# One word of each row of the first raw weights is fetched ahead of everything else, with the order of all engines drawn up anew

## The chip, the cores and the metric

The kernel runs on one core of a Trainium2 chip. A core has engines with instruction queues of their own: TensorE (PE: matmuls, and PEld for its weight loads), VectorE (DVE), ScalarE (ACT), GpSimd (POOL) and SyncE (SP), which here issues every DMA. The metric is the device time of one execution in microseconds (us), the median of repeated runs. The kernel before has 666.44 us.

## What is computed

Attention between 512 tokens and 32 states per head, both ways, for 8 batches of 8 heads of width 64. Then all 4,352 rows go through a gated product: two matmuls with 512 x 1536 weights, an elementwise product, and a matmul with 1536 x 512 weights.

```python
def _attn_ref(x, state):
    scores = scale * np.matmul(x, state.transpose(0, 1, 3, 2))
    a = softmax(scores)                       # over the 32 states
    xread = np.matmul(a, state)
    scores2 = scale * np.matmul(state, x.transpose(0, 1, 3, 2))
    a2 = softmax(scores2)                     # over the 512 tokens
    sread = np.matmul(a2, x)
    return np.concatenate([xread, sread], axis=2)

def reference(x, state, moe_w_a, moe_w_b, moe_w_out):
    x = _attn_ref(x, state) as rows of 512
    return ((x @ moe_w_a) * (x @ moe_w_b)) @ moe_w_out
```

## The kernel before

Every product is kept near float32 by splitting its operands into a high and a low part of 11 to 12 bits (names ending in `_h` and `_l`) and adding three products: high by high, high by low, low by high. Weights arrive as raw 64-bit words (`wl` for the first layer, `w_out` for the second). A conversion turns each 512 KB piece of them into float32: ScalarE makes `t1` from the raw words (`pre`), and VectorE follows with two shifts with masks, a multiply-add and a sum (`Whole.run`), or with a few more where the high and low parts are wanted apart (`Conv.run`). The trace writes such tiles as `raw` or, where the buffer has another name, `sd_h` and `sd_l`, the shifted words as `t`, and converted weights as `wo`.

The start of the program is this chain, for batch 0. The tokens `x` arrive in two halves for the first four heads (`x<-xt`, two transfers of 288 KB), then in one of 576 KB for the others. `scores` multiplies them with the states into the PSUM tile `ms`. ScalarE copies that (`p_raw`), TensorE turns it back to rows of tokens (`acc<-ident,p_raw`), and VectorE takes the maximum `m` of each group and subtracts it (`s_p`). ScalarE exponentiates, VectorE adds and divides, TensorE transposes again, and ScalarE splits the result into `sd_h` and `sd_l` (batch 0 has its attention weights in these buffers; later batches in `at_h` and `at_l`). Meanwhile the four pieces of the first two chunks of `wl` are converted, and `direct` multiplies them with the states into `p_h` and `p_l`. Layer 1 (`layer1`, `product`) multiplies these with the attention weights into two PSUM tiles `ab`, and their elementwise product is `a_sb`, with parts `g_h` and `g_l`. Layer 2 multiplies `g` with `wo0`, `wo1` and so on into `acc`. From then on eight batches and twelve such pieces of the hidden width follow; the last part works with seven products in place of eight for blocks of two by two (`sevens`).

Until the first layer-1 matmul TensorE also runs 80 matmuls `ab<-y` whose result nobody reads. They fill its idle time (`WARM`, `COLD`).

The order of the instructions is not that of the code. Every call is recorded as a unit with an engine, a duration and its dependences; `plan` then simulates the engines with these costs and always starts the ready unit that is due first. Due times are worked out backwards from the end and moved by two tables of numbers found by search: `SHIFTS` moves the due time of a group of units, `RELEASES` holds a group back until a given time. The result is one fixed order on each engine, and the semaphores follow from it. The cost of a load is an issue on SP, a start-up, a time for its bytes and a fixed time to land; `Conv.load` gives the very first piece of `wl` an extra cost. Each engine runs its queue in the order planned: an instruction that waits holds up all behind it.

All instructions are issued by one line of code at the end (L1800), so in the trace they are told apart by their tiles.

Of the kernel before, what the change touches and what calls it, by code (L numbers as in the profile page):

```python
# [12 lines left out]
I32 = mybir.dt.int32  # L13
# [7 lines left out]
P = 128  # L21
# [26 lines left out]
T0, PACE = 15e3, 1.12  # L48
STARTS = {}
# [246 lines left out]
class Engine:  # L296
# [557 lines left out]
def attn_moe(ctx, tc, xt, xn, sd, wl, w_out, out):  # L854
# [20 lines left out]
    tail = pool("tail", 8)  # L875
# [41 lines left out]
    class Conv:  # L917
# [6 lines left out]
        def load(self, place):  # L924
            self.raw = load64(self.src, place, self.runs)
            if not count[0]:
                u = rec.units[-1]
                u.serve, u.land, u.lat = u.serve + 1200, u.land + 900, u.lat + 2100
# [914 lines left out]
```

## Time and profile before

| | |
|---|---|
| median of 3 runs (lowest, highest) | 666.44 us (665.91, 666.53) |
| the profiled execution | 665.95 us |
| its span, first to last instruction | 663.7 us |
| TensorE busy | 653.6 us (98%) |
| VectorE busy | 548.5 us (83%) |
| ScalarE busy | 382.0 us (58%) |
| 16 DMA engines busy, mean | 70% |
| granted TensorE clock, mean | 0.999 |

The profiled execution lies 2.25 us above its span and 0.49 us below the median of the runs. Busy time of TensorE is an upper measure, since a matmul's record overlaps the next one's by up to some 0.16 us; waits of less than that do not show as idle time. The rest is read by stage.

### The profile page before, as it was taken

The numbers are of one execution on the slowest core, as the hardware profiler recorded it, in microseconds if no ns is written. First come the engines' busy times: TensorE is split into PE (matmuls) and PEld (weight loads), VectorE is DVE, ScalarE is ACT, GpSimd is POOL, SyncE is SP. The second block draws the span as 40 slices with busy tenths as digits, with TensorE's granted clock in tenths as the row PEclk, the third lists the DMA queues.
The fourth block names the chain that finished last, engine by engine and source line by source line (L and its number), as shares of the span: only waits on it lengthen the run. The fifth ranks groups of instructions, "written<-read, shape, count | busy, mean of one in ns | idle before, by whom it ended". The sixth has DMA issues, their size and how long they took to land.

```text
span 663.7 us, 12125 instructions
## 1 busy us (share of the span) xinstructions
PE 653.6 (98%) x4451; PEld 544.9 (82%) x4451; DVE 548.5 (83%) x1219; ACT 382.0 (58%) x707; POOL 0.7 (0%) x6
## 2 busy tenths in 40 slices
PE   7999999999999999999999999999999999999997
PEld 4566777776777778888888989898989989889996
DVE  5999989998877787878989978877777879877885
ACT  4677488699989976654545543534444444424442
POOL 0000000000000000000000000000000000000000
PEclk9999999999999999999999999999999999999999
DMA  8998579889989999866876764754426217268830
GB/s 298 356 359 310 232 252 343 285 308 359 351 296 391 339 325 344 314 213 187 253 239 217 249 231 121 251 169 159 156 100 168 98 53 213 75 181 188 233 96 33
DMA packets 77242, 155.06 MB, mean 234 GB/s; under 512 B 7040, under 2 KB 26240, under 8 KB 77184
## 3 DMA queue, kind: packets, MB, share of 16 engines
q1 hardware_dynamic: 77184, 154.30, 69.7%
q8 instruction: 35, 0.57, 0.4%
q14 instruction: 23, 0.19, 0.1%
HBM read 91.36 MB, written 62.91 MB: 232 GB/s over the span
## 4 chain that ended last, share of the span: by engine, by line
PE 91%; DVE 5%; DMA 1%; ACT 1%; issue 1%; DVEq 0%
PE ab L1800 44%; PE acc L1800 39%; PE ms L1800 9%; DVE t L1800 2%; DVE wo L1800 1%; DMA x<-xn 1%; DVE m L1800 1%; DVE s_p L1800 1%; DMA x<-xt 0%; DVE stg L1800 0%; DVE p_l L1800 0%; DVE g_l L1800 0%; ACT sw_st L1800 0%; ACT g_h L1800 0%; DVE x L1800 0%
## 5 line engine op out<-in xcount | busy, mean ns | idle before, releaser
L1800 PE MATMUL acc<-wo,g_h 128*128 128x256 f32 (+1 forms) x868 | 178.8, 316 | 0.6 <-ACT stg L1800 0.3
L1800 PEld LDWEIGHTS acc<-wo,g_h 128*128 128x128 f32 x868 | 135.4, 190 | 19.9 <-issue 3.4
L1800 PE MATMUL ab<-at_l,p_h 128*128 128x512 f32 x368 | 144.5, 393 | 0.0
L1800 PE MATMUL ab<-at_h,p_h 128*128 128x512 f32 x368 | 144.4, 397 | 0.0
L1800 PE MATMUL ab<-at_h,p_l 128*128 128x512 f32 x368 | 143.2, 391 | 0.0
L1800 PE MATMUL acc<-wo,g_l 128*128 128x256 f32 (+1 forms) x587 | 127.3, 308 | 0.2
L1800 PEld LDWEIGHTS acc<-wo,g_l 128*128 128x128 f32 x587 | 93.0, 190 | 11.5 <-issue 1.2
L1800 ACT CAST g_h<-a_sb 128x512 fp32r<-128x512 f32 (+1 forms) x104 | 63.8, 613 | 56.7 <-DVE a_sb L1800 26.9
L1800 PEld LDWEIGHTS ab<-at_h,p_h 128*128 128x128 f32 x368 | 69.1, 188 | 17.5 <-issue 2.9
L1800 PEld LDWEIGHTS ab<-at_h,p_l 128*128 128x128 f32 x368 | 69.1, 188 | 15.7 <-issue 0.8
L1800 PEld LDWEIGHTS ab<-at_l,p_h 128*128 128x128 f32 x368 | 69.3, 188 | 12.1 <-issue 0.8
L1800 DVE TENSOR_TENSOR g_h<-a_sb,g_h 128x512 fp32r<-128x512 f32 x68 | 46.5, 684 | 15.8 <-PE acc L1800 11.7
L1800 ACT COPY wq<-ab 128x512 f32<-128x512 f32 (+1 forms) x48 | 27.3, 568 | 43.5 <-PE ab L1800 43.4
L1800 DVE TENSOR_TENSOR wq<-ab,wq 128x512 f32<-128x512 f32 (+1 forms) x48 | 31.9, 664 | 21.9 <-PE ab L1800 19.0
L1800 ACT CAST p_h<-p_raw 128x1024 fp32r<-128x1024 f32 x32 | 33.6, 1051 | 21.9 <-PE ab L1800 18.8
L1800 DVE TENSOR_TENSOR p_l<-p_raw,p_h 128x1024 fp32r<-128x1024 f32 x32 | 38.9, 1214 | 1.3 <-ACT p_h L1800 1.2
L1800 DVE TENSOR_TENSOR stg<-acc,stg 128x256 f32<-128x256 f32 (+1 forms) x68 | 36.3, 549 | 3.6 <-PE acc L1800 2.6
L1800 ACT CAST g_l<-wq 128x384 fp32r<-128x384 f32 x46 | 23.5, 513 | 26.6 <-PE acc L1800 23.9
L1800 DVE TENSOR_TENSOR g_l<-wq,g_l 128x384 fp32r<-128x384 f32 x46 | 25.4, 552 | 15.4 <-PE acc L1800 10.7
L1800 ACT COPY p_raw<-ms 128x512 f32<-128x512 f32 x48 | 27.6, 590 | 10.5 <-PE ms L1800 9.8
L1800 DVE TENSOR_SCALAR t<-t 128x512 int32<-128x512 int32 x64 | 26.7, 418 | 5.1 <-ACT t L1800 4.8
L1800 DVE TENSOR_TENSOR a_sb<-ab,a_sb 128x512 f32<-128x512 f32 (+1 forms) x36 | 23.6, 654 | 7.1 <-PE ab L1800 5.4
(137 smaller groups left out, 1060.0 us busy)
## 6 DMA issues: line engine op xcount, KB each, us to landing
p_raw<-scr SPq DMA_DIRECT2D x32, 512.0 KB, 4.8
raw<-wl SPq DMA_DIRECT2D x20, 512.0 KB, 5.3
out<-stg SPq DMA_DIRECT2D x33, 256.0 KB, 2.2
su<-wq SPq DMA_DIRECT2D x16, 512.0 KB, 6.0
scr<-sw_st SPq DMA_DIRECT2D x32, 256.0 KB, 4.7
scr<-p_raw SPq DMA_DIRECT2D x32, 256.0 KB, 4.7
x<-xn SPq DMA_DIRECT2D x16, 512.0 KB, 5.0
x<-xt SPq DMA_DIRECT2D x14, 512.0 KB, 6.4
```

The source lines that it names most:

```text
L1800: getattr(obj, method)(*map(real, args), **{k: real(x) for k, x in kw.items()})
```

## The change

Three things are edited. A DMA `touch<-wl` is issued first: 8 bytes of each of 128 rows of `wl[0]` (two 32-bit words, 1 KB in all) into a small tile that nobody reads. The two loads of batch 0's first tokens are recorded as users of that tile, which puts them behind it in the order, without a wait. And the planner's extra cost of the first load of weights is cut to a fifth. Both tables were then searched anew, so the order of every engine changes along the whole program.

```diff
 T0, PACE = 15e3, 1.12
+TOUCHED = True
...
 SHIFTS = {
-    0: 961, 1: 522, 2: -345, 3: -1004, 4: 175, 5: 340, 6: 86993674, 7: 86992534, 8: -40, 9: 377, 10: -272, 11:
...
         def load(self, place):
             self.raw = load64(self.src, place, self.runs)
             if not count[0]:
                 u = rec.units[-1]
-                u.serve, u.land, u.lat = u.serve + 1200, u.land + 900, u.lat + 2100
+                u.serve, u.land, u.lat = u.serve + 200, u.land + 200, u.lat + 400
...
+    touch = tail.tile([P, 2], I32, name="touch", bufs=1)
+    nc.sync.dma_start(out=touch, in_=wl[0, :, 0, :1].bitcast(I32))
...
                 if self.b == 0 and g == 0:
                     for h in range(2):
-                        nc.sync.dma_start(out=x[:, g, h], in_=xt[self.b, g, :, h])
+                        u = nc.sync.dma_start(out=x[:, g, h], in_=xt[self.b, g, :, h])
+                        u.touch.append(touch)
+                        u.acc.append((touch.tile, 0, False))
```

The instructions on TensorE, VectorE and ScalarE are the same ones before and after, in another order; SP has one DMA more. Three places show the order.

On SP, the first transfers of the program, before:

```order
L1800 DMA x<-xt 128x576 x2
L1800 DMA raw<-wl 128x1024
L1800 DMA x<-xt 128x1152
L1800 DMA raw<-wl 128x1024
L1800 DMA sd_h_122<-wl 128x1024
L1800 DMA kept_0_128<-p_raw 128x512
L1800 DMA xst<-sd 64x4x128 x2
L1800 DMA sd_l_144<-wl 128x1024
L1800 DMA x<-xt 128x2x512 x2
```

and now (the first row is the new transfer, `kept` stores the scores, `xst` are the states):

```order
L1807 DMA touch<-wl 128x2
L1807 DMA x<-xt 128x576 x2
L1807 DMA raw<-wl 128x1024 x2
L1807 DMA x<-xt 128x1152
L1807 DMA xst<-sd 64x4x128 x2
L1807 DMA kept_0_145<-p_raw 128x512
L1807 DMA sd_h_149<-wl 128x1024
L1807 DMA sd_l_164<-wl 128x1024
```

The new transfer stands first, so each `x` moves back by one issue. The third piece of weights (`sd_h<-wl`) stood ahead of the store `kept<-p_raw`, which waits for ScalarE; it now stands behind it, and the second piece has moved ahead of the third load of `x`.

On TensorE, its first rows (`ab<-y` are the matmuls that nobody reads, `ms<-x` the first scores), before:

```order
L1800 MATMUL ms<-x 32x512 x4
L1800 MATMUL ab<-y 128x256 x3
L1800 MATMUL acc<-ident,p_raw 128x128 x4
L1800 MATMUL ab<-y 128x256 x14
L1800 MATMUL ms<-x 32x512 x4
L1800 MATMUL ab<-y 128x256 x12
L1800 MATMUL acc<-ident,s_p 128x128 x4
```

and now:

```order
L1807 MATMUL ab<-y 128x256 x12
L1807 MATMUL ms<-x 32x512 x4
L1807 MATMUL ab<-y 128x256 x5
L1807 MATMUL acc<-ident,p_raw 128x128 x4
L1807 MATMUL ab<-y 128x256 x10
L1807 MATMUL ms<-x 32x512 x4
L1807 MATMUL ab<-y 128x256 x13
L1807 MATMUL acc<-ident,s_p 128x128 x4
```

Twelve of the unread matmuls now stand ahead of the first scores; before, TensorE began with the scores.

On VectorE, its 48th to 58th instructions, around the first two products `a_sb` of layer 1 (`wo_413` and `wo_403` are the same piece of weights under two numbers), before:

```order
L1800 TENSOR_TENSOR a_sb<-ab,a_sb 128x512
L1800 TENSOR_TENSOR wo_413<-wo_413,t_399 128x512
L1800 TENSOR_SCALAR t_428<-t_417 128x512
L1800 TENSOR_SCALAR wo_413<-t_417 128x512
L1800 SCALAR_TENSOR_TENSOR t_428<-sd_l_314,t_428 128x512
L1800 TENSOR_TENSOR wo_413<-wo_413,t_428 128x512
L1800 TENSOR_TENSOR g_l<-a_sb,g_h 128x512
L1800 TENSOR_SCALAR t_460<-t_447 128x512
L1800 TENSOR_SCALAR wo_466<-t_447 128x512
L1800 SCALAR_TENSOR_TENSOR t_460<-raw,t_460 128x512
L1800 TENSOR_TENSOR a_sb<-ab,a_sb 128x512
```

and now:

```order
L1807 TENSOR_TENSOR wo_403<-wo_403,t_398 128x512
L1807 TENSOR_TENSOR a_sb<-ab,a_sb 128x512
L1807 TENSOR_SCALAR t_440<-t_431 128x512
L1807 TENSOR_SCALAR wo_403<-t_431 128x512
L1807 SCALAR_TENSOR_TENSOR t_440<-sd_l_326,t_440 128x512
L1807 TENSOR_TENSOR wo_403<-wo_403,t_440 128x512
L1807 TENSOR_SCALAR t_459<-t_437 128x512
L1807 TENSOR_SCALAR wo_465<-t_437 128x512
L1807 SCALAR_TENSOR_TENSOR t_459<-raw,t_459 128x512
L1807 TENSOR_TENSOR g_l<-a_sb,g_h 128x512
L1807 TENSOR_TENSOR a_sb<-ab,a_sb 128x512
```

The first `a_sb` has moved behind one sum of weights and the first `g_l` behind three instructions of the next piece; the second `a_sb` is the 58th instruction in both. The first 58 instructions are the same set in both orders, as are the first 64 and the first 150.

## Rows read from the trace of the kernel before

**Rows 1.** Page, part 1: busy us of each engine, its share, instructions.

```profile
PE 653.6 (98%) x4451; PEld 544.9 (82%) x4451; DVE 548.5 (83%) x1219; ACT 382.0 (58%) x707; POOL 0.7 (0%) x6
```

**Rows 2.** Chain that ended last, 0 to 45 us: start us, us, what.

```profile
0.73 2.96 DMA x<-xt
...
3.73 2.59 PE ms L1800 x8
...
35.74 0.61 DVE a_sb L1800
...
36.38 0.63 ACT g_h L1800
...
37.05 2.11 PE acc L1800 x8
```

**Rows 3.** What VectorE waited for, 0 to 41 us: total us, times, longest.

```profile
DVE m L1800 <- PE acc L1800: 7.8, 1, 7.8
```

**Rows 4.** Windows, all engines: length, busy us (x instructions) of each, clock, DMA share, GB/s.

```profile
7.78:24.96 17.18, 15.51 (x139) 11.55 (x137) 16.97 (x36) 8.50 (x16) 0.00 (x0) 1.00 1.01 380
...
24.96:41.14 16.18, 15.85 (x94) 9.96 (x94) 16.01 (x33) 10.75 (x23) 0.00 (x0) 1.00 0.89 312
```

**Rows 5.** Timeline, 0.7 to 8.6 us: start, us, engine, line, operation [idle before].

```profile
0.73 0.86 SPq L1800 DMA_DIRECT2D x<-xt  x2
...
1.65 0.42 SPq L1800 DMA_DIRECT2D raw<-wl  x1
...
2.03 0.31 ACT L1800 ACTIVATE y<-ident 128x128 fp32r<-128x128 f32 x1
...
4.40 0.18 PEld L1800 LDWEIGHTS ms<-x 64*32 64x32 f32 x4 [0.48 <-DMA x<-xt]
...
6.37 0.59 ACT L1800 COPY p_raw<-ms 128x512 f32<-128x512 f32 x1 [4.03 <-PE ms L1800]
...
6.85 0.67 ACT L1800 ACTIVATE t<-raw 128x512 f32<-128x512 f32 x1
```

**Rows 6.** Timeline of TensorE, 0 to 45 us.

```profile
9.34 1.06 PE L1800 MATMUL ms<-x 64*32 64x512 f32 x8
...
10.33 1.70 PE L1800 MATMUL ab<-y 128*128 128x256 f32 x12
...
24.96 0.50 PE L1800 MATMUL ab<-sd_h,p_h 128*128 128x512 f32 x1 [0.47 <-ACT p_h L1800]
```

**Rows 7.** Windows of half a us, while the first transfers run.

```profile
3.00:3.50 0.50, 0.00 (x0) 0.00 (x0) 0.00 (x0) 0.00 (x0) 0.00 (x0) 1.00 1.04 410
...
5.50:6.00 0.50, 0.50 (x4) 0.00 (x0) 0.00 (x0) 0.00 (x0) 0.00 (x0) 1.00 0.34 95
```

**Rows 8.** DMA issues of two short windows (1.6 and 8.7 us): KB, us to landing.

```profile
raw<-wl SPq DMA_DIRECT2D x1, 512.0 KB, 5.1
...
sd_l<-wl SPq DMA_DIRECT2D x1, 512.0 KB, 5.0
```

**Rows 9.** Timeline of VectorE, 0 to 45 us.

```profile
9.11 0.42 DVE L1800 TENSOR_SCALAR t<-t 128x512 int32<-128x512 int32 x1
...
19.63 0.67 DVE L1800 TENSOR_TENSOR wo<-wo,t 128x512 f32<-128x512 f32 x1
...
20.31 0.70 DVE L1800 STREAM_TRANSPOSE s_p<-p_raw 128x512 f32<-128x512 f32 x1
...
21.07 0.66 DVE L1800 TENSOR_REDUCE m<-s_p 128x16 f32<-128x512 f32 x1
```

**Rows 10.** What TensorE waited for, 41 to 664 us.

```profile
PE acc L1800 <- ACT stg L1800: 0.3, 1, 0.3
...
PE acc L1800 <- DVE stg L1800: 0.2, 1, 0.2
```

**Rows 11.** Chain that ended last, two pieces of short matmuls.

```profile
390.97 3.00 PE acc L1800 x23
...
525.14 2.99 PE acc L1800 x25
```

727 rows, old and new, of tables (RELEASES, SHIFTS) are left out of this document.

## The prediction

> **What bounds the kernel now.** I read the page first. TensorE is busy for 98% of the span [rows 1], so nearly all of the time is matmuls, and those are the same before and after. A change of order can win only where TensorE has nothing useful to do: at the start, and in small waits later. I then took the chain that ended last in its first 45 us [rows 2]. It runs from the first tokens, 0.73 to 3.69 us, through the scores on TensorE, 3.73 to 6.32, and then for 29 us mostly over VectorE, up to the second product `a_sb` at 35.74; ScalarE makes `g_h` from it at 36.38, and the layer-2 matmuls that need it start at 37.05. From there the chain stays on TensorE.
>
> So the start is bound by VectorE. Two views say how tightly. It waits once in the first 41 us, 7.8 us for the transposed scores [rows 3], and is then busy for 16.97 of 17.18 us and 16.01 of 16.18 us [rows 4]: 0.38 us of gaps in 33. No instruction of it waited for a weight. After 41 us TensorE waits visibly for 0.5 us in all [rows 10].
>
> **The change, part by part.**
>
> *Weights sooner.* The first piece is issued at 1.65 [rows 5] and lands 5.1 us later [rows 8], at 6.75. ScalarE takes it up at 6.85, right behind the copy of the scores that began at 6.37 [rows 5], and is done at 7.52. VectorE first uses it at 9.11 [rows 9], behind the maximum and the subtraction of the scores. The new order on VectorE begins with the same rows, scores first. What hides an earlier landing is thus 9.11 - 7.52 = 1.59 us of slack that exists already: an earlier first piece gains nothing, and one up to 1.5 us later would cost nothing. If that cover were gone, each us would count in full. The time that the planner no longer charges was not on the path.
>
> *The tokens later.* SP spends 0.86 us on two issues [rows 5], so one more in front costs 0.43 us, and the second half of `x`, which TensorE had at 4.40 [rows 5], comes at 4.83. How much longer the touch itself holds it no row shows, so I bound it. Below: nothing more. Above: the touch now meets whatever slowed the first piece of weights. From the second half of `x` at 4.40, 512 KB at the 410 GB/s of the queue at 3.0 to 3.5 us [rows 7] would have been in at 5.68; it was in at 6.75, so 1.07 us were lost, and the queue moved 95 GB/s at 5.5 to 6.0 although that piece was still under way [rows 7]. With all of that in front of `x`, its second half comes at 5.90.
>
> Later packets did stand still behind slow ones, as far as the 95 GB/s [rows 7] show. The Trainium skill's page "DMA: Bandwidth & Descriptors" says, under "Two DMAs through the same engine are not ordered", that descriptors of one queue start in order but are pipelined. By that rule `x` would not be held at all and come at 4.83; by the row it could come at 5.90. The trace agrees with the rule only in part.
>
> *Twelve unread matmuls in front of the scores.* They need `y`, done at 2.03 + 0.31 = 2.34 [rows 5]. Twelve took 1.70 us in the first stretch at the full 2.4 GHz [rows 6]. The level is read from durations, since the clock column shows 1.00 throughout [rows 7]: the eight score matmuls that took 2.59 us at 3.73, TensorE's first work [rows 2], took 1.06 at 9.34 [rows 6], after it had been running. At 1.2 GHz the twelve take up to 3.4 us less the tail of the last, so the scores can begin at 5.0 to 5.5; I take 5.2. This covers `x` at 4.83. The scores then take 1.06 us if the clock is up, and twice that, 2.12, if not. TensorE starts its work 1.3 us sooner than before, so I take 1.5: they end at 6.7, against 6.32, which is +0.4. Ends: 5.0 + 1.06 = 6.06, or -0.3; and 5.90 + 2.12 = 8.02, or +1.7.
>
> *What the shift does.* The path from the scores over copy, transposes and VectorE's 58 instructions to the second `a_sb` is the same set of work. The copy and transposes follow as before (7.8 - 6.32 = 1.48 us), and VectorE has at most 0.38 us of gaps to win. So the layer-2 matmuls of 37.05 start at 37.45, and as TensorE is full from there, the +0.4 stays to the end.
>
> *The reordered start.* The second half of batch 0's softmax is normalised before four VectorE instructions that stood ahead of it: a shift like the one at 9.11 (0.42), a sum (0.67), a transpose (0.70), a maximum (0.66) [rows 9], 2.45 us of records or some 2.1 us of queue, since each overlaps the next by 0.08. The first layer-1 matmul, which had waited for `p_h` until 24.96 [rows 6], may start up to 2.1 us sooner. I cost that at nothing: the four instructions still come before the 58th, and TensorE only waits longer for it.
>
> *Third and fourth piece of weights.* They now stand behind the store of the scores, which waits for ScalarE's copy (6.96, now 7.4). Behind it in SP's queue are both pieces and the next batch's tokens. Issued at about 8 and 8.5 and landing after the 5.0 us of the fourth piece before [rows 8], they come at 13 and 13.5. VectorE reaches the third behind 16 instructions, most of 0.42 to 0.70 us [rows 9], so some 8 us after its start, at about 16. It is covered by 2 us.
>
> *Everything after 45 us.* The work is the same in a new order, the last matmuls follow their last `g_h` behind the same nine others, and only waits can differ. What there is: 0.5 us in two visible waits [rows 10], and holes too small to see as idle. One such: 23 short matmuls took 3.00 us where 25 took 2.99 [rows 11], a hole of 0.25 us. I bound the new order by six holes fewer or more, 1.5 us each way, and take nothing; that is a choice.
>
> **The sum.** 665.95 us of the profiled execution + 0.4 - 0 (weights) - 0 (earlier layer 1) + 0 (rest) = 666.35. The median of the runs shown lies 0.49 us above the profiled execution, so I predict 666.8 us. A difference of 0.2%, 1.33 us, is about what a measurement of this kernel can tell from no change.
>
> **Rivals.**
>
> 1. *The earlier layer 1 counts after all:* 666.8 - 2.1 = 664.7. For it: TensorE did wait for `p_h` at 24.96. Against it: the second `a_sb` gates at 37.05, and VectorE had 0.38 us to spare. It holds if VectorE's start is not what orders that stretch. Chance 0.10.
>
> 2. *The new tables have fewer holes later:* six fewer give 665.3, and with the scores at the early end 664.6. For it: a new search sets the order of 600 us of TensorE. Against it: only 0.5 us of that shows as waiting. Chance 0.17.
>
> 3. *Slower, `x` held behind the touch:* the first scores end at 8.02 and everything is 1.7 us later, 666.44 + 1.7 = 668.1. It decides from an end of the scores at 6.32 + 1.33 = 7.65. For it: the queue that stood at 95 GB/s. Against it: the twelve matmuls cover `x` until 5.2, and the clock should be up by then. Chance 0.13.
>
> 4. *Slower later:* six holes more, 668.3, or the second piece of `w_out`, now issued behind a store that waits for VectorE's sum, lands too late for ScalarE, which has the conversion of it queued ahead of `p_h`. Chance 0.10.
>
> 5. *No measurable change, the forecast:* 0.50.
>
> That makes 0.27 for faster by over 0.2%, 0.50 for within 0.2%, 0.23 for slower. The range reaches to the faster rivals' 664.7 and to the slower ones' 668.3. The forecast's own range is 665.9 to 667.8.
>
> **What would show it.** In the changed profile VectorE should start at 8.2 (7.5 to 9.5) and still wait once, for the transposed scores. The second `a_sb` should stand 28 us behind that, at about 36.1, and the layer-2 matmuls at 37.45. The first weights should land in under 5.1 us and still be used after the scores. The first layer-1 matmul may stand near 23, with more waiting behind it. The forecast is wrong if VectorE starts before 7.5, if the second `a_sb` comes earlier than 35 with TensorE full behind it, or if TensorE's waits after 41 us differ from 0.5 us by more than a us.

## The result, and the profile after

The changed kernel takes 672.34 us (median of 4 executions, 671.52 to 672.58), the kernel before 666.49 us on the same chip: ratio 1.0087, 95% interval 1.0070 to 1.0105. The forecast was no change. The profiled execution took 672.19 us with a span of 670.4, against 665.95 and 663.7 before.

First the page, part 1, of the changed kernel (busy us, share, instructions), to set beside [rows 1].

```profile
PE 655.5 (98%) x4451; PEld 546.2 (81%) x4451; DVE 550.3 (82%) x1219; ACT 382.0 (57%) x707; POOL 0.7 (0%) x6
```

The same work, 1.9 us more of it by the record, and the span is 6.7 us longer: the loss is in waits and in slower stretches. What VectorE waited for up to 42 us (total us, times, longest), which was one line in [rows 3]:

```profile
DVE m L1807 <- PE acc L1807: 8.8, 1, 8.8
DVE t L1807 <- ACT t L1807: 0.9, 1, 0.9
DVE s_p L1807 <- ACT p_raw L1807: 0.4, 1, 0.4
```

It starts at 8.82 instead of 7.78, and then waits twice more, 1.35 us in all. The chain that ended last says what is behind the first of them (start us, us, what), where [rows 2] had VectorE from 7.8 us on:

```profile
2.39 2.93 PE ab L1807 x12
5.32 1.86 PE ms L1807 x8
...
8.82 0.70 DVE m L1807
...
15.11 0.70 DVE wo L1807
15.83 0.43 SPq L1807
...
16.31 9.37 DMA raw<-w_out
...
25.79 0.66 ACT t L1807
26.45 0.26 ACT p_h L1807
...
27.25 0.50 PE acc L1807
```

At 15.11 VectorE makes a sum of weights. SP stores it at 15.83, and only behind that store issues the second piece of `w_out`, which takes 9.37 us. ScalarE converts it at 25.79, and `p_h` stands behind that conversion. TensorE waits for `p_h`, and VectorE for the converted piece. The sum itself follows from VectorE's start alone: VectorE runs without a wait from 8.82 to 15.11. Why the load behind it took so long is seen in the timeline of SP (start, us to issue) and in the second scores on TensorE:

```profile
0.73 0.39 SPq L1807 DMA_DIRECT2D touch<-wl  x1
...
2.11 0.91 SPq L1807 DMA_DIRECT2D raw<-wl  x2
3.06 0.43 SPq L1807 DMA_DIRECT2D x<-xt  x1
...
13.33 1.23 SPq L1807 DMA_DIRECT2D x<-xt  x2
...
15.30 0.36 SPq L1807 DMA_DIRECT2D raw<-w_out  x1
15.83 0.43 SPq L1807 DMA_DIRECT2D sf<-wo  x1
16.31 0.43 SPq L1807 DMA_DIRECT2D raw<-w_out  x1
```

```profile
5.25 1.93 PE L1807 MATMUL ms<-x 64*32 64x512 f32 x8
...
12.21 1.06 PE L1807 MATMUL ms<-x 64*32 64x512 f32 x8 [2.24 <-DMA x<-xt]
```

The third load of `x` goes out at 3.06, behind both pieces of raw weights, and the second scores start at 12.21 instead of 9.34 [rows 6]. SP issues the next batch's tokens (`x<-xt x2`) when these scores are done, at 13.33, and both pieces of `w_out` behind them. In the kernel before, the same loads stand here:

```profile
10.46 1.21 SPq L1800 DMA_DIRECT2D x<-xt  x2
11.78 2.64 SPq L1800 DMA_DIRECT2D raw<-w_out  x2
```

The second `a_sb` and its `g_h`, at 35.74 and 36.38 in [rows 2], now stand here (timelines of VectorE and ScalarE):

```profile
38.56 0.68 DVE L1807 TENSOR_TENSOR a_sb<-ab,a_sb 128x512 f32<-128x512 f32 x1
```

```profile
25.79 0.66 ACT L1807 ACTIVATE t<-raw 128x512 f32<-128x512 f32 x1 [1.30 <-DMA raw<-w_out]
26.35 0.36 ACT L1807 CAST p_h<-acc 128x256 fp32r<-128x256 f32 x1
...
39.28 0.62 ACT L1807 CAST g_h<-a_sb 128x512 fp32r<-128x512 f32 x1
```

That is 2.9 us later: 1.0 from VectorE's start, 1.35 from its waits, and some 0.5 from gaps too small to be listed. The rest is in what TensorE waited for after 41 us, two lines and 0.5 us in [rows 10]:

```profile
PE ms L1807 <- DVE p_l L1807: 0.9, 1, 0.9
PE ab L1807 <- ACT a_sb L1807: 0.6, 1, 0.6
PE ab L1807 <- DVE u_c L1807: 0.5, 1, 0.5
PE acc L1807 <- ACT u_c L1807: 0.5, 1, 0.5
PE ms L1807 <- ACT p_raw L1807: 0.3, 1, 0.3
PE acc L1807 <- DVE m L1807: 0.3, 1, 0.3
```

That is 3.1 us in six waits, each at a place of its own. I also counted, for each profiled execution, the time of a matmul less the useful matmuls done before it (each shape at its usual spacing, unread ones at nothing). Set against the profile of the kernel before, the changed kernel is by that count 2.8 us behind after 40 us of useful work, 3.9 after 160, 5.1 after 300 and 6.1 at the last matmul; the end after it is 0.6 us longer.

### The profile page after: what moved, and what is told of

Read it like the earlier page. It is cut to its first block, busy times and chain, and to the rows that moved or that the text cites. A ratio compares the mean times of both kernels' runs of the same rounds, so it can differ in the third digit from the quotient of the medians.

```text
span 670.4 us, 12147 instructions
## 1 busy us (share of the span) xinstructions
PE 655.5 (98%) x4451; PEld 546.2 (81%) x4451; DVE 550.3 (82%) x1219; ACT 382.0 (57%) x707; POOL 0.7 (0%) x6
## 4 chain that ended last, share of the span: by engine, by line
PE 82%; DMA 6%; DVE 5%; ACT 5%; issue 1%; SPq 0%; DVEq 0%; ACTq 0%
PE ab L1807 41%; PE acc L1807 34%; PE ms L1807 7%; DMA raw<-w_out 1%; ACT wq L1807 1%; DMA p_raw<-sd 1%; DMA scr<-p_raw 1%; DVE t L1807 1%; DVE m L1807 1%; DMA kept<-p_raw 1%; DMA scr<-sw_st 1%; DMA out<-stg 1%; DMA stg<-part 1%; ACT t L1807 1%; ACT p_raw L1807 1%
## 5 line engine op out<-in xcount | busy, mean ns | idle before, releaser
L1807 PE MATMUL acc<-wo,g_h 128*128 128x256 f32 (+1 forms) x868 | 181.9, 316 | 0.5 <-DVE m L1807 0.3
L1807 PE MATMUL acc<-wo,g_l 128*128 128x256 f32 (+1 forms) x587 | 130.6, 308 | 0.0
L1807 PEld LDWEIGHTS acc<-wo,g_l 128*128 128x128 f32 x587 | 94.8, 190 | 11.6 <-issue 1.2
```

The costliest lines, as they stand in the source:

```text
L1807: getattr(obj, method)(*map(real, args), **{k: real(x) for k, x in kw.items()})
```

## The experiments

In all but the changed kernel itself the order is written out:

```diff
-    order, start = plan(rec.units, pools, T0)
+    order = ORDER
```

Below, OLD and NEW are the two orders, and OLD_41 and NEW_41 their parts up to the last gate matmul of the first layer, at about 41 us. A ratio is to the kernel before on the same chip, with its 95% interval.

**Which part loses.** Four kernels split the change.

```diff
+touch_alone:  ORDER = [touch] + OLD
+tables_alone: ORDER = NEW without touch
+start_before: ORDER = OLD_41 + what is left, in NEW's order
+start_after:  ORDER = NEW_41 + what is left, in OLD's order
```

> The order of the kernel before on every engine, with the touch as SP's first transfer. Theory A (the loss at the start comes from the order of the loads, not from the touch): the touch costs one SP issue, 0.4 us on x, and little else; 0.3 to 0.9 us slower than before, VectorE starts at 8.1 to 8.5, the third load of x lands before 10 us. Theory B (the touch itself slows the first transfers): 2 us slower or more, the third load of x after 11 us. Theory C (the touch quickens the first weights, and the tables hide it): not slower, first weights in 4.5 us or less.

Measured 1.0009 [1.0000, 1.0019], 0.77 us by the medians: theory A. The timeline shows `x` just one issue later, and the first weights no sooner:

```profile
4.00 0.19 PEld L1752 LDWEIGHTS ms<-x 64*32 64x32 f32 x4 [4.00 <-DMA x<-xt]
...
4.86 0.18 PEld L1752 LDWEIGHTS ms<-x 64*32 64x32 f32 x4 [0.67 <-DMA x<-xt]
...
8.77 0.68 ACT L1752 ACTIVATE t<-raw 128x512 f32<-128x512 f32 x1 [1.36 <-DMA raw<-wl]
```

The second half comes at 4.86, against 4.40 [rows 5]. ScalarE waits 1.36 us for the raw weights, which came at 6.75 before and at 8.7 now. That much is also found without the touch: the first piece took 5.1 to 7.2 us in seven profiles without it (start_before had 7.2) and 4.9 to 7.6 in thirteen with it, with a median of 5.7 in both.

> The order of the changed kernel on every engine, without the touch. Theory A: 5.0 to 5.6 us slower than before, x's third load still lands some 9 us after its issue and the second piece of w_out still holds p_h at 26 us. Theory B: the start is as before, only the later 3.3 us of waits remain, so 3 to 3.6 us slower. Theory C: slower than the changed kernel by 0.5 us or more, since the first weights come later.

Measured 1.0079 [1.0062, 1.0096], 5.4 us by the medians: nearly all of the loss, without the touch, as theory A has it.

> The order of the kernel before up to the last layer-2 matmul of the second piece (some 41 us), then the order of the changed kernel for all that is left; no touch. At this point both orders have done the same set of work. Theory A with two losses (2.5 us at the start, 3.3 us of waits and holes spread over the rest): 2.8 to 3.9 us slower than before. Theory D (the later waits follow from the late start): within 1 us of before.

Measured 1.0052 [1.0035, 1.0070], 3.2 us by the medians: theory A.

> The order of the changed kernel with the touch up to the same point, then the order of the kernel before. Theory A with two losses: 2.2 to 3.0 us slower than before. Theory D: 5 us slower or more, since whatever follows a late start waits too.

Measured 1.0045 [1.0028, 1.0063], 2.8 us by the medians: theory A. By the count of useful work it is 2.6 us behind at 40 us and 2.5 at the last matmul. So there are two losses which add, one before 41 us and one behind it, and the touch is little of either.

**The start.** Four edits of start_after.

```diff
+x3_early, SyncE:
 raw<-wl (first piece)
+x<-xt (third load)
 raw<-wl (second piece)
-x<-xt (third load)
+pad_moved, TensorE: 20 of the 29 ab<-y from 15.65 us go to just before acc<-p_h,y
+pad_behind, TensorE: the first 12 ab<-y go behind the first ms<-x
+p_h_first, ScalarE: p_h, sd_h go ahead of t<-raw (second w_out)
```

> Base: the kernel with the new order up to the first layer's last gate matmul and the old order behind it (start_after: ratio 1.0045, its second scores at about 12.2 us, 2.9 us of waiting for p_h). One edit on SyncE: the third load of x (all of the second 576 KB) goes out ahead of the second piece of raw weights, as in the kernel before. Theory A (the order of the first loads holds the start): it lands near 9.5 to 10, the second scores start at 9.6 to 10.4, the next x, the second raw w_out and with it p_h come 1.5 to 2.5 us sooner, the wait for p_h falls under 1.2 us, and the ratio falls to 1.001 to 1.002. Rival B (the path to w_out is held by the raw weights or VectorE, the third x only has slack): the second scores move sooner, the wait for p_h stays over 2 us and the ratio stays at 1.0035 to 1.005.

Measured 1.0012 [1.0003, 1.0021], as theory A has it. The second scores start at 9.29, and VectorE waits only once, as before the change; the second `a_sb` stands at 36.03 instead of 38.18 in start_after. What VectorE waited for up to 42 us, then rows of TensorE, SP and ScalarE:

```profile
DVE m L1752 <- PE acc L1752: 8.2, 1, 8.2
...
9.29 1.06 PE L1752 MATMUL ms<-x 64*32 64x512 f32 x8
...
10.42 1.22 SPq L1752 DMA_DIRECT2D x<-xt  x2
...
15.60 0.43 SPq L1752 DMA_DIRECT2D raw<-w_out  x1
...
22.64 0.67 ACT L1752 ACTIVATE t<-raw 128x512 f32<-128x512 f32 x1 [1.24 <-DMA raw<-w_out]
```

The second `w_out` is issued 7.4 us behind VectorE's start in both kernels (15.60 here, 16.44 in start_after), since in both it stands behind the store of the sum. But it takes 6.9 us here and 9.1 there. The next batch's tokens went out 2.8 us sooner, and the queue moved 410 GB/s from 10 to 17 us, against 307 (the last number; start_after first):

```profile
10.00:17.00 7.00, 5.14 (x43) 4.09 (x43) 6.86 (x15) 3.68 (x6) 0.00 (x0) 1.00 0.86 307
10.00:17.00 7.00, 5.86 (x49) 5.37 (x46) 6.86 (x15) 3.75 (x7) 0.00 (x0) 1.00 1.06 410
```

Of the 2.15 us between the two `a_sb`, 1.24 are VectorE's later waits, which are gone; 0.84 are an earlier start of VectorE, at 8.21 instead of 9.05. The profiles do not show that the moved row makes that start earlier.

> Same base. Twenty of the 29 unread 256-column matmuls ahead of the third scores (15.65 to 19.3 us) move to just ahead of the first matmul that waits for p_h (2.75 us of wait). Theory A with the clock as a second part: TensorE is busy for 2.2 of the 2.75 us, the granted clock does not fall to the lower level at 28 to 31.6 us, the 512-column matmuls there stay near 0.23 us apart, and about 1.4 us come back: ratio 1.002 to 1.003. Rival C (the clock's fall is covered by VectorE, which gates a little later): the clock stays up, and a wait of 1 us or more for a_sb or g_h appears instead; ratio 1.004 to 1.005.

Measured 1.0034 [1.0022, 1.0046], within the interval of start_after, so the times do not tell A from C. The profiles do: start_after's own granted clock was 1.00 at 28 to 32 us, and its second `a_sb` (38.18) was nearly as late as that of the changed kernel (38.56). The clock that fell to 0.61 and 0.54 in the changed kernel (below) cost little of this. With the unread matmuls in that gap, TensorE's wait for `p_h` is 0.5 us, and 0.5 us for `a_sb` and 0.9 us of issue come instead; `a_sb` comes at 37.66, still behind 1.24 us of VectorE's waiting for `t`.

```profile
28.00:30.00 2.00, 2.00 (x7) 1.63 (x7) 2.00 (x5) 2.00 (x6) 0.00 (x0) 0.61 1.05 407
30.00:32.00 2.00, 2.00 (x13) 1.02 (x11) 2.00 (x5) 0.43 (x1) 0.00 (x0) 0.54 0.96 319
```

(Windows of the changed kernel; the third number from the end is the granted clock.)

> Same base. The twelve unread matmuls that lead TensorE go behind the first scores. Theory A: the first scores start with x near 3.5 to 4 us and VectorE 0.8 to 1.3 us sooner (7.5 to 8.0 us instead of 8.8), but the wait for p_h hangs on the second raw w_out, so the ratio stays within 0.001 of 1.0045. Rival D (the later start of the first scores is what the start loses): VectorE's gain goes through to the gate, and the ratio falls to 1.0025 to 1.003.

Measured 1.0052 [1.0040, 1.0064]. The edit did more than it was for: the twelve came to stand between the scores and their transposes, at the lower of the two clock levels (213 ns apart), and VectorE started at 11.35. It tells nothing on D, but something else: with no later wait over 0.3 us, the second `a_sb` stood 28.0 us behind that start.

> Same base. On ScalarE the copies p_h and sd_h0 go ahead of t1 of the second raw w_out (which waits for its load until 25.7 us). Theory A in the form of the prediction's fourth rival (queued ahead of p_h on ScalarE): p_h is ready near 24.4 us, TensorE goes on about 2 us sooner, the clock does not fall, and of the loss of the start 1.5 to 2.5 us come back: ratio 1.0005 to 1.002. Rival E (w_out itself is on VectorE's path to the next shift): the wait only moves to wo or a_sb, 1.5 to 2.5 us there, and the ratio stays at 1.0035 to 1.005.

Measured 1.0031 [1.0019, 1.0043], between A and E. `p_h` was waited for 0.4 us only, but VectorE waited for `p_raw` (1.1), `m` (0.5) and `t` (0.5), and its second `a_sb` came at 38.91. The early `p_h` did not move the gate; that is E's side.

VectorE's start, its waits behind it, and its second `a_sb` in the profiled executions, in us, with the last column worked out as `a_sb` less the two others:

| kernel | start | waits | a_sb | rest |
|---|---|---|---|---|
| before | 7.78 | 0 | 35.66 | 27.9 |
| touch_alone | 8.50 | 0 | 36.36 | 27.9 |
| x3_early | 8.21 | 0 | 36.03 | 27.8 |
| pad_behind | 11.35 | 0.23 | 39.38 | 27.8 |
| pad_moved | 8.43 | 1.24 | 37.66 | 28.0 |
| start_after | 9.05 | 1.24 | 38.18 | 27.9 |
| tables_alone | 9.09 | 2.0 | 39.33 | 28.2 |
| p_h_first | 8.65 | 2.07 | 38.91 | 28.2 |
| after | 8.82 | 1.35 | 38.56 | 28.4 |

Nine kernels, one and the same 28 us of VectorE, and the eleven other profiles give 27.8 to 28.2 as well. VectorE gates the start, and what makes it late is its first input and the inputs that it waits for later, of weights or scores.

**The rest, and one try at a faster kernel.**

```diff
+mid_seam:  ORDER = OLD up to about 300 us + what is left, in NEW's order
+p_l_first: start_before; VectorE's p_l at 132 us goes ahead of five raw<-raw
+lead_six:  OLD; y and six ab<-y go ahead of the first ms<-x
```

> The order of the kernel before up to about 300 us of the span, the new order behind it, no touch. Theory A (the rest of the loss is a row of single waits, each made by the rows around it): only those that lie behind 300 us come (acc for u_c at 328, ab for u_c at 652, the longer tail), and by the useful work done up to each moment the loss is 1.0 us up to the last matmul and 0.6 behind it: 1.4 to 1.9 us, ratio 1.0020 to 1.0030. Rival F (the new tail is as good, and the loss comes from what the new start of the rest sets off): ratio under 1.0012.

Measured 1.0034 [1.0022, 1.0046]: above A's range, but with an interval that reaches into it, and not into F's. Behind 300 us TensorE waits for `u_c` three times (0.5 each) and for `m` (0.3).

> Base: the old order up to the first layer's last gate matmul and the new order behind it (start_before: ratio 1.0052). One edit on VectorE: the subtraction that makes p_l (132 us, the one TensorE waits 0.9 us for) goes ahead of the five raw<-raw subtractions that stand before it. Theory A: that wait falls under 0.2 us, nothing takes its place, ratio 1.0036 to 1.0044. Rival G (VectorE is full there, so that the five come later and their reader waits instead): a wait of 0.5 us or more at another place between 130 and 180 us, ratio 1.0048 to 1.0056.

Measured 1.0042 [1.0028, 1.0057]. The wait is gone, and `at_l`, now behind on VectorE, is waited for instead (TensorE's waits, 120 to 180 us):

```profile
PE ab L1752 <- DVE at_l L1752: 0.4, 1, 0.4
PE ms L1752 <- ACT p_raw L1752: 0.3, 1, 0.3
```

In start_before VectorE was busy for all of 126 to 134 us: G's mechanism. The time lies in A's range, but start_before itself came out at 1.0030 later, so no gain of this row is shown.

> The order of the kernel before, no touch, with one edit: y and six of the unread matmuls go ahead of the first scores, so that TensorE starts near 2.4 us instead of 3.73 and the scores can still start when x has landed, near 3.7 to 3.9 us. Theory A (VectorE's start sets the start, and the clock's rise does not follow TensorE's start): VectorE starts between 7.8 and 8.6 us and the ratio is 0.999 to 1.001. Rival H (the step of the prediction: TensorE 1.3 us sooner brings the clock 1.3 us sooner): clock up by 6 us, VectorE starts by 7.3 us, ratio 0.9988 to 0.9995.

Measured 0.9998 [0.9990, 1.0007], in A's range; the interval also reaches into H's. The clock decides: the scores took 2.16 us from 3.96, at the lower level, so it was not up by 6 us, as H needs. VectorE started at 7.56, between the two forecasts. No version here beats the kernel before.

**The two losses put together.**

```diff
+two_rows, two_rows_2: NEW with x3_early's row and p_l_first's row
+whole_same: ORDER = NEW
+x3_whole: NEW with x3_early's row
+start_before_2: as start_before
+g_h_first: x3_early; ScalarE's cast g_h (second gate) ahead of s_p and p_raw
+g_h_whole: x3_whole with the same move
```

> The changed kernel whole (touch and new order from end to end, ratio 1.0087) with two rows moved: the third load of x ahead of the second raw piece on SyncE, and p_l at 132 us ahead of the five raw<-raw on VectorE. Theory A (the losses add): 1.8 to 2.2 us come back from the first and 0.8 to 1.0 from the second, ratio 1.0036 to 1.0050. Rival I (the two hide each other, or the start's loss in the whole kernel is not that of the third x): ratio 1.0058 or more.

Measured 1.0073 [1.0056, 1.0089]; its executions spread from 668.84 to 672.37. Theory A's size is outside the interval.

> The changed kernel as it is, its order written out instead of planned, on the same chip as the three kernels beside it. Theory A (the third x costs about 2 us in the whole kernel too, and what came back in two_rows was too little because single executions differ by up to 3.5 us): 1.0080 to 1.0095, with executions spread by 2 to 3.5 us. Rival I (the third x costs little in the whole kernel): the same number; told apart by the difference to x3_whole.

Measured 1.0079 [1.0066, 1.0092], spread 2.6 us. Its profile shows how much the start itself varies: in the same order as the changed kernel, VectorE's waits are 0.6 us instead of 1.35, and the second `a_sb` stands at 37.15 instead of 38.56.

> The changed kernel whole with the third load of x ahead of the second raw piece, and nothing else. Theory A: 1.6 to 2.4 us less than whole_same, ratio 1.0050 to 1.0068. Rival I (in the whole kernel the wait only moves to the loads of the middle, p_raw<-scr near 260 us): under 1 us less than whole_same, ratio 1.0072 or more.

Measured 1.0068 [1.0055, 1.0080]: 0.44 us less than whole_same, where the same row gave 2.1 us with the old rest. In the profiles VectorE's later waits fall from 0.6 us to none and its second `a_sb` moves from 37.15 to 36.43, so there was less to win than in start_after.

> The same program as two_rows. Theory A: 0.5 to 1.0 us less than x3_whole, ratio 1.0040 to 1.0060. Rival I: as the first time, 1.0065 to 1.0080, within 0.5 us of x3_whole.

Measured 1.0064 [1.0049, 1.0079], nearer to I. Its profile shows why one row is not a sure cure. Issued at 2.58 as in x3_early, the third load of `x` landed 9.3 us later, not 6.6:

```profile
11.95 1.47 PE L1752 MATMUL ms<-x 64*32 64x512 f32 x8 [2.84 <-DMA x<-xt]
```

> The same program as start_before (old order up to the first layer's last gate matmul, new order behind it). It gives the loss of the rest on the same chip: theory A 1.0045 to 1.0056, and whole_same minus this, 2 to 3 us, is what the start loses. Rival J (the rest loses more in some executions, by the loads of the middle, so that its ratio isn't a constant): executions spread by over 2.5 us and a ratio outside of 1.0045 to 1.0056.

Measured 1.0030 [1.0018, 1.0042], against 1.0052 the first time, with a spread of only 1.0 us. The ratio is outside theory A's 1.0045 to 1.0056, as J has it, but without J's spread. The two profiles show where such a difference can arise. The one of start_before is its slowest execution (671.17); by the count of useful work the two are 0.2 us apart at 160 us, and 2.9 at 300. Between these a load `p_raw<-scr`, issued at 260.54 and 260.63, takes 7.1 us in the first and 4.0 in the second, and ScalarE waits for it (start_before's row first). Behind it, TensorE in start_before waits for ScalarE's `wq` (third row), a wait that start_before_2 does not have:

```profile
267.69 1.05 ACT L1752 CAST p_h<-p_raw 128x1024 fp32r<-128x1024 f32 x1 [4.80 <-DMA p_raw<-scr]
264.69 1.05 ACT L1752 CAST p_h<-p_raw 128x1024 fp32r<-128x1024 f32 x1 [2.06 <-DMA p_raw<-scr]
269.28 0.50 PE L1752 MATMUL ab<-at_h,p_h 128*128 128x512 f32 x1 [1.16 <-ACT wq L1752]
```

The profile of two_rows, also its slowest execution, has the same: ScalarE waits 4.4 us for this load and TensorE 0.8 for `wq`.

> Base x3_early (new start with the third x early, old rest, ratio 1.0012). One edit on ScalarE: the cast g_h that TensorE's second gate matmuls of the first layer wait for goes ahead of the activation s_p and the copy p_raw that stand before it; in x3_early it starts 0.65 us after VectorE's a_sb is done, in the kernel before at once. Theory K (with the third x repaired, ScalarE's order ahead of this gate is what the start still loses): the cast starts within 0.1 us of a_sb's end, 0.5 to 0.7 us come back, ratio 1.0000 to 1.0006. Rival L (the remaining 0.0012 is the touch's delay of VectorE's start): ratio 1.0008 to 1.0018.

> Base x3_whole (the changed kernel with the third x early, ratio 1.0068), the same edit on ScalarE. Theory K: 0.4 to 0.8 us come back, ratio 1.0055 to 1.0064, and what is left is the loss of the rest. Rival M (the middle takes it back, by the transfers near 260 us): ratio 1.0065 to 1.0080.

Measured 1.0026 [1.0017, 1.0035] and 1.0062 [1.0049, 1.0075]. Both changed part of the computation: in the written order the cast came to stand ahead of VectorE's addition to `a_sb`, so it reads the part before the sum, and the addition waits for it (1.0 and 0.8 us, a wait of VectorE's ahead of its second `a_sb`). Theory K is therefore untested. What the first does show is once more the gate: with a third load that also came late (0.7 us of VectorE's waits for `t` and `s_p`), `a_sb` moved from 36.03 to 37.53, and the time rose by 0.0014.

## Why the prediction was wrong

**Right: VectorE gates the start.** Its work up to the second `a_sb`, "the same set of work", took 27.8 to 28.4 us in every profile. That such a delay "stays to the end" holds only for a large one: start_after, 2.6 us behind at 40 us of useful work, is 2.5 behind at the last matmul, but touch_alone, 0.7 behind up to 80, is level with the kernel before from 240 on. (That profile, of 665.78 us, is its fastest execution; its median is 0.77 us slower.)

**Right: the touch.** The tokens came 0.46 us later for a forecast of 0.43. The Trainium skill's page "DMA: Bandwidth & Descriptors" says, under "Two DMAs through the same engine are not ordered", that descriptors start in order but are pipelined; the prediction took from it that `x` is not held and comes at 4.83, and the 4.86 of touch_alone agrees. The bound of 5.90 was not reached. Rival 3 fell: the first scores ended at 7.18, before its 7.65. That the first weights "should land in under 5.1 us" was wrong, at no cost: they took 6.4 us in the changed kernel, within the spread that they have without the touch.

**Right in the middle, partly by luck: the twelve unread matmuls.** The term was +0.4; in the changed kernel's profile VectorE starts 1.04 us later. The twelve took 2.93 us and the scores 1.86 in the chain, where I had chosen 1.5 between 1.06 and 2.12: in this profile TensorE's earlier start did not bring the faster clock level forward. Twelve profiles of this same beginning on TensorE show 1.06 to 1.93 us for these scores, median 1.87, and put VectorE's start at 7.78 to 9.09 us, median 8.6, within the 7.5 to 9.5 of the prediction; five of the old beginning without the touch have 7.78 to 8.42, median 8.2. By the medians the term is the +0.4 of the forecast; the one profiled execution of before was an early one.

**Failed: the loads.** The third and fourth piece of weights were covered, as "Third and fourth piece of weights" has it. But that was all that I asked of SP's new order. In the same rows the third `x` moved behind the second raw piece, and got no term. It holds the second scores, hence the next batch's tokens, which SP issues when these scores are done (13.33 instead of 10.46), and hence the two pieces of `w_out` behind them: the second took 9.4 us in the changed kernel and 6.8 in two_rows, issued at the same moment (16.31 and 16.30) with the third `x` early. Its late arrival at ScalarE is the second half of rival 4, which was named, given little weight, and not priced by itself; but the rival saw the store as the reason, and x3_early keeps the store and loses VectorE's wait. VectorE's later waits were forecast at none and are 1.35 us in the changed kernel. In x3_early one row of SP takes them away, and the ratio falls from 1.0045 to 1.0012; part of that fall, 0.8 us in the profiles, is VectorE's earlier start there, which varies by as much between profiles of one order of TensorE. Rival 1 went the other way: the first layer-1 matmul, which "may stand near 23", came at 27.58 instead of 24.96 [rows 6].

**Also covered: TensorE's wait for `p_h` and the clock that fell behind it.** They look like the cause in the chain, 2.7 us of idle TensorE and then a slower stretch, but filling the gap (pad_moved) and clearing it (p_h_first) did not bring the second `a_sb` nearer to VectorE's start: it came 29.2 and 30.3 us behind it, against 29.1 in start_after.

**Failed: "Everything after 45 us ... take nothing", bounded by 1.5 us.** It costs 2.0 to 3.5 us (start_before_2 1.0030, start_before 1.0052), and the prediction's own sign of being wrong, TensorE's waits over a us away from 0.5, was met. The bound came from holes of 0.25 us in the old order, and these say nothing of what a new order may hold: six waits of 0.3 to 0.9 us, 3.1 us in all, in the changed kernel. Why one wait is not easily cured is seen in p_l_first: VectorE is full there. The chain near the end shows the same kind, where [rows 11] had TensorE alone:

```profile
650.79 0.44 DVE stg L1807
...
651.25 0.44 DVE u_c L1807
...
651.71 1.29 DVE stg L1807 x2
652.99 0.34 DVE u_c L1807
...
653.47 1.64 PE ab L1807 x8
```

The addition to `u_c` stands behind two sums of the output on VectorE, and TensorE waits 0.5 us for it.

**Open.** The losses add up roughly: 1.0045 and 1.0030 to 1.0052 make 1.0075 to 1.0097, and the whole measured 1.0079 and 1.0087. But the third `x` gave back 0.0033 with the old rest and 0.0011 with the new one, and each of these differences is uncertain by about 0.002, which is what separates them. Two things that vary between executions are seen in the profiles: what VectorE waits for in one and the same start (1.35 and 0.6 us), and the load near 260 us: between 160 and 300 us of useful work the new rest lost 0.5 us in the profile in which it took 4.0 us, and 3.2 in the one in which it took 7.1. A third suspect is a row of ScalarE: in x3_early, x3_whole and two_rows `g_h` stands 0.65 us behind `a_sb`'s end. Whether the row is really worth less in the whole kernel was not settled. Nor do two profiles settle why start_before gave two ratios; they show one load that can make such a difference. Of the six later waits only one was taken out alone, and no gain was shown, so what each of them costs stays open.

## What to carry to other kernels

A new order has to be read on every queue as far as its first late consumer: each row that moved, the loads too, gets a term of its own, above all the row that the change is not about. Where one engine gates a stretch, ask of every input of that engine when it now comes, and not only of the input that was meant to come sooner. And a new order of 600 us of a full engine is not neutral because the old one had no waits: here that part alone cost 2 to 3.5 us, and bounds from the old order's holes were too narrow. When single profiles are compared, a difference of the size of their own spread (here 1.3 us in VectorE's start alone) is not the change's.

## What the hardware showed

- A read of 1 KB spread over the rows of `wl` did not make the first large load from it faster: the first piece took 5.7 us in the median of thirteen profiles with it and of seven without. The queue moved 205, 197 and 229 GB/s at 5.0 to 6.5 us in the changed kernel, against 318 at 3.0 to 3.5.
- How long one and the same load takes differs from one execution to the next: the third `x`, issued at 2.58 us behind the same transfers, took 6.6 us in x3_early and 9.3 in two_rows_2, and `p_raw<-scr`, issued near 260.6 us, 7.1 in start_before and 4.0 in start_before_2.
- TensorE's clock rose at moments that did not follow its start. With its first matmul at 2.39 us, the first scores at 5.25 took 1.06 us in g_h_first, 1.48 in x3_early and 1.93 in the changed kernel; the 256-column matmuls went from 213 ns apart (1.2 GHz) to some 120 (2.4 GHz) by 6.9 us in x3_early and 8.1 in the changed kernel; in the kernel before, which began at 3.73, the transposes were already 110 ns apart at 7.3.
